# SiLU as one ScalarE function, a compact attention state, and later fills of the buckets, in a one-core attention and expert kernel

## The chip, the core and the metric

The kernel runs on one core of one Trainium2 chip. Its engines are TensorE (PE, with weight loads shown as PEld), VectorE (DVE), ScalarE (ACT), GpSimd (POOL) and SyncE (SP), which issues most transfers. The metric is the time of one execution on the device in microseconds; lower is better. A time of the kernel is a median of several runs; the profile shows one more execution by itself, whose time is given beside its span.

## The reference

Three stages follow each other. The state of the first is 48 x 48 for each of 4 x 8 heads; x then has 3072 rows (tokens) of 384.

```python
# 1: attention with a decayed state; q, k, v, alpha: (4, 8, 768, 48)
for t in range(768):
    state = alpha[:, :, t, :, None] * state + k[:, :, t] (x) v[:, :, t]
    y[:, :, t] = q[:, :, t] @ state
# 2: x: (3072, 384); w_gate, w_val: (384, 1536); w_out: (1536, 384)
xn = x / sqrt(mean(x * x) + 1e-6) * rms_g
g = xn @ w_gate
x = (g / (1 + exp(-g)) * (xn @ w_val)) @ w_out
# 3: one of 8 experts for each row; w1: (8, 384, 1024); w2: (8, 1024, 384)
logits = x @ r_gate
e = argmax(logits);  p = exp(logits - max);  p = p / (sum(p) + 1e-9)
out[row] = p[e] / (1 + exp(-(x @ r_ogate)[e])) * (relu(x @ w1[e]) @ w2[e])
```

The weights of stage 2 arrive as 64-bit floats.

## The kernel before

**Tiles.** The 768 steps of a batch are cut into six chunks of 128, so that there are 24 tiles of 128 rows. Three tiles make a group of 384 rows, and there are eight groups. A tile of attention has five stages: `score` (products `ps_s` of keys and queries, 16 matmuls, masked by DVE into `P0` and `P1`), `ktr` (keys turned on PE, copied by ACT to `kn`), `outp` (`ps_y`: queries times the old state plus the masked scores times `v`, then the RMS norm), `state` (`ps_st`: keys times values, added to the state) and `xtr` (the normed rows turned, and split by ACT and DVE into a high part `xh` and a rest `xl`, which PE multiplies separately). Ahead of `score` stands the preparation of a tile: loads `blk_a`, `blk_q`, `blk_k`, a turn of `alpha` on DVE (`aT`, L340), a running product, and scaled `qT`, `kT` and `en`, the decay over the whole chunk.

**The state.** Each tile of the state is [128, 4, 96]: four pairs of heads, of which the first head of a pair has partitions 0 to 47 and columns 0 to 47, the second partitions 64 to 111 and columns 48 to 95; the remainder is zero, so that one matmul serves a pair. POOL fills three such tiles with zeros at the start (L188). In `score`, DVE multiplies the state by `en`, one instruction for each of the two blocks (L393). In `state`, DVE adds `ps_st` block by block (L454), or, for the first chunk of a batch, DVE or ACT copies it (L450, L452).

**Stage 2** works on blocks of 128 of the 1536 inner columns, 12 for each group, so 96 in all. `m_gate` makes `ps_g` with nine matmuls (L571); ACT writes tanh(g/2) to `tt` (L562), and DVE makes (tt + 1) g of it (L563). `m_val` makes `ps_v`; DVE multiplies tt by half of it (L582) and ACT copies the result to its high part `hh` (L585). `m_low` takes the rest `hl` on DVE (L591). `m_out` multiplies both by the block of `w_out`, nine matmuls of 400 columns (L605), in which the last three read `hl`; it adds up in three banks `ps_o`.

**Weights of stage 2.** They are loaded as pairs of 32-bit words (`stg`, L485), converted by DVE in three operations (the first of them L490) into a buffer `F` or `Fo` (three of them, under the tag `cF`), and split by ACT and DVE. This is finished some 170 us into the run. For that reason the first two groups are interleaved: runs s = 0 to 3 are group 0 blocks 0 to 5, group 1 blocks 0 to 5, group 0 blocks 6 to 11, group 1 blocks 6 to 11. From then on a group is one run.

**Routing.** `route_a` of a group takes the maximum and the exponentials of 8 logits per row, and the output gate as exp(-o), in short operations on DVE and ACT; `route_b` counts rows on PE, makes the rows' places `pos`, and POOL scatters the rows into `bucket` in DRAM (eight regions, one for each expert). `init_bucket` fills a region beforehand with empty rows by one transfer on SP (L689) from `zrow`. Group 0 is routed in run 3, each later group in the run behind its own, and the last one behind everything. Then stage 3 loads rows of an expert (`er`, L956), turns them on PE and multiplies (`ps_h` L571, `ps_b` L1007).

**What sets the order.** The program is written in loops that interleave stages by due times; the first tiles follow a list in `CFG['START']`. A scheduler then places the instructions of each engine by simulated times, except for some that are pinned to the written order. Fills are pinned, at these lines of the loop over run s and step n, one for every second step of run 2:

```python
if s == 2 and (n - CFG['IB']) % 2 == 0 and 0 <= (n - CFG['IB']) // 2 < E:
    init_bucket((n - CFG['IB']) // 2)
```

Of the kernel before, what the change touches and what calls it, by code (L numbers as in the profile page):

```python
# [8 lines left out]
F32 = mybir.dt.float32  # L9
# [3 lines left out]
AF = mybir.ActivationFunctionType  # L13
# [38 lines left out]
def gla_glu_moe_kernel(  # L52
# [16 lines left out]
    nc = tc.nc  # L69
# [114 lines left out]
    place_of = [(t % BS, t // BS) if t < BS * NCH else (BS, t - BS * NCH) for t in range(NTILE)]  # L184
    state_of = []
    for i in range(BS):
        t_ = att.tile([P, NP, 2 * D], F32, name=f"state{i}")
        nc.gpsimd.memset(t_, 0.0)  # L188
        state_of.append(t_)

    vt = {}
    pre = {}
# [59 lines left out]
    def seat_of(t, nm, shape, bufs=1):  # L252
        if (t, nm) in SIDE:
            tag, i = SIDE[t, nm]
            if tag not in side:
                side[tag] = wpool.tile([P, 3, NP * P], F32, tag=tag, name="side")
            flat = side[tag][:, i, 0:shape[1] * (shape[2] if len(shape) > 2 else 1)]
            return flat.rearrange("p (a b) -> p a b", a=shape[1]) if len(shape) > 2 else flat
        return att.tile(shape, F32, tag=nm, name=nm, bufs=bufs)
# [113 lines left out]
    def stages(t):  # L373
        b, c = place_of[t]
        first, final = c == 0, c == NCH - 1
        en, qT, kT = pre[t]
        S_ = state_of[b % BS]
        rs = [slice(64 * hh, 64 * hh + D) for hh in range(2)]
        ds_ = [S_[rs[hh], :, hh * D:hh * D + D] for hh in range(2)]
        g, ti = divmod(t, GT)  # L380
        Pt = {}

        def score():
            ps = [bank([P, NP, P], "ps_s") for _ in range(2)]
            for p in range(NP):
                for hh in range(2):
                    r = slice(64 * hh, 64 * hh + D)
                    nc.tensor.matmul(ps[hh][:, p, :], lhsT=kT[r, p, :], rhs=qT[r, p, :], start=True, stop=True)  # L388

            def post():  # L390
                if not first:
                    for hh in range(2):
                        nc.vector.tensor_tensor(out=ds_[hh], in0=ds_[hh], in1=en[rs[hh]].to_broadcast([D, NP, D]),  # L393
                                                op=ALU.mult)
                mb = mask.to_broadcast([P, NP, P])
                for hh in range(2):
                    Ph = seat_of(t, f"P{hh}", [P, NP, P])
                    pace(f'Ph{t}', nc.vector.tensor_tensor(out=Ph, in0=ps[hh], in1=mb, op=ALU.mult))
                    Pt[hh] = Ph
            return post  # L400
        yield score

        def ktr():
            if final:
                return None
            ps = bank([P, NP, P], "ps_k")
            for p in range(NP):
                nc.tensor.transpose(ps[:, p, :], kT[:, p, :], ident)  # L408
            kn = seat_of(t, "kn", [P, H, D])
            nc.scalar.activation(kn, ps.rearrange("p a (h d) -> p (a h) d", h=2)[:, :, 0:D], AF.Copy)  # L410
            Pt["kn"] = kn
            return None
        yield ktr
# [23 lines left out]
        def state():  # L437
            if final:
                return None
            kn = Pt["kn"]  # L440
            ps = bank([P, NP, D], "ps_st")
            for p in range(NP):
                for hh in range(2):
                    nc.tensor.matmul(ps[64 * hh:64 * hh + D, p, :], lhsT=kn[:, 2 * p + hh, :],  # L444
                                     rhs=vt[t][:, 2 * p + hh, :], start=True, stop=True)

            def post():
                for hh in range(2):
                    if first and b < BS and SM[b] == "a":
                        nc.scalar.activation(ds_[hh], ps[rs[hh]], AF.Copy)  # L450
                    elif first:
                        nc.vector.tensor_copy(ds_[hh], ps[rs[hh]])  # L452
                    else:
                        nc.vector.tensor_tensor(out=ds_[hh], in0=ps[rs[hh]], in1=ds_[hh], op=ALU.add)  # L454
            return post
        yield state

# [97 lines left out]
    def m_gate(g, j):  # L555
        xh, xl = xT[g]
        ps = psM.tile([P, G], F32, tag="g", name="ps_g")
        mm3(ps, weight("wgh", j), weight("wgl", j), xh, xl)

        def post():  # L560
            tt = act.tile([P, G], F32, tag="t", name="tt")
            nc.scalar.activation(tt, ps, AF.Tanh, scale=0.5)  # L562
            nc.vector.scalar_tensor_tensor(out=tt, in0=tt, scalar=1.0, in1=ps, op0=ALU.add, op1=ALU.mult)  # L563
            hbuf[g, j] = tt
        return post

# [8 lines left out]
    def m_val(g, j):  # L575
        xh, xl = xT[g]
        ps = psM.tile([P, G], F32, tag="v", name="ps_v")
        mm3(ps, weight("wvh", j), weight("wvl", j), xh, xl)

        def post():  # L580
            tt = hbuf[g, j]
            nc.vector.scalar_tensor_tensor(out=tt, in0=tt, scalar=0.5, in1=ps, op0=ALU.mult, op1=ALU.mult)  # L582
            hh = act.tile([P, G], F32R, tag="hh", name="hh")
            hl = act.tile([P, G], F32R, tag="hl", name="hl")
            nc.scalar.activation(hh, tt, AF.Copy)  # L585
            hbuf[g, j] = (hh, hl, tt)
        return post
# [42 lines left out]
    def route_a(g):  # L630
# [6 lines left out]
        nc.vector.tensor_tensor(out=ex, in0=L, in1=mx.to_broadcast(bc), op=ALU.subtract)  # L637
        oh = small("oh", bc)
        nc.vector.tensor_scalar(out=oh, in0=ex, scalar1=0.0, scalar2=None, op0=ALU.is_ge)
        nc.scalar.activation(ex, ex, AF.Exp)  # L640
        nc.vector.tensor_tensor(out=oh, in0=oh, in1=rev8.to_broadcast(bc), op=ALU.mult)
        m8 = small("m8", [P, GT, 1])
        nc.vector.tensor_reduce(out=m8, in_=oh, op=ALU.max, axis=AX.X)
# [8 lines left out]
        nc.vector.tensor_tensor(out=sg, in0=oh, in1=O, op=ALU.mult)  # L652
        og = small("og", [P, GT, 1])
        nc.vector.tensor_reduce(out=og, in_=sg, op=ALU.add, axis=AX.X)
        nc.scalar.activation(og, og, AF.Exp, scale=-1.0)
        se = small("se", [P, GT, 1])
        nc.vector.tensor_reduce(out=se, in_=ex, op=ALU.add, axis=AX.X)
        rt[g] = (oh, ohb, ohc, m8, og, se)
# [1 line left out]
    def route_b(g):  # L660
# [6 lines left out]
            nc.tensor.matmul(ps[:, i, :], lhsT=ones_b, rhs=ohc[:, i - 1, :], start=False, stop=True)  # L667
        nc.tensor.matmul(ps[:, GT, :], lhsT=ones_b, rhs=ohc[:, GT - 1, :], start=True, stop=True)
        bc = [P, GT, E]
        nc.vector.tensor_scalar(out=se, in0=se, scalar1=1e-9, scalar2=None, op0=ALU.add)  # L670
        nc.vector.scalar_tensor_tensor(out=se, in0=og, scalar=1.0, in1=se, op0=ALU.add, op1=ALU.mult)
        nc.vector.reciprocal(out=R[:, :, DM:DM + 1], in_=se)
        nc.vector.tensor_copy(R[:, :, DM + 1:DM + 2], tokid[:, g * GT:g * GT + GT, :])
        rk = small("rk", bc)
        nc.vector.tensor_tensor(out=rk, in0=ps[:, 0:GT, :], in1=cnt.to_broadcast(bc), op=ALU.add)
# [11 lines left out]
    def init_bucket(e):  # L687
        tc.keep_in_program_order(
            nc.sync.dma_start(bucket[e * REG:e * REG + CMAX, :].rearrange("(p b) w -> p b w", p=P),  # L689
                              zrow.to_broadcast([P, CMAX // P, RW])))  # L690


    chunks = weight_chunks()
# [40 lines left out]
    def prep_step():  # L734
        if prep:
            prep.pop(0)()
# [91 lines left out]
    for s in range(4):  # L828
        N = 3 * (runs[s][2] - runs[s][1])
        paced[0] = CFG['K2'] if s else CFG['K1']  # L830
        for n in range(N):
# [22 lines left out]
            if s == 0 and done % NST == 0:  # L854
                while prep:
                    prep_step()
            if s == 2 and (n - CFG['IB']) % 2 == 0 and 0 <= (n - CFG['IB']) // 2 < E:
                init_bucket((n - CFG['IB']) // 2)
            if s == 3 and n == CFG['RA0']:
                route_a(0)  # L860
            if s == 3 and n == CFG['RB0']:
                route_b(0)


    BIG = float(1 << 20)
# [161 lines left out]
    for g in range(2, NG):  # L1027
# [14 lines left out]
        for n in range(3 * KF):  # L1042
# [3 lines left out]
            if done < (NTILE - GT) * NST and ((g - 1) * 3 * KF + n + 1 + CFG['LEADG']) * GT >= (done + 1 - GT * NST) * 3 * KF / NST:  # L1046
                post = stage()
                if post:
                    post()
            prep_step()  # L1050
            if n == CFG['RA']:
                route_a(g - 1)
            if n == CFG['RB']:
# [261 lines left out]
```

## Time and profile before

| | |
|---|---|
| three timed runs | 896.6, 899.89, 901.41 us (median 899.89) |
| the profiled execution | 895.87 us, of it 894.2 us span |
| busy in it: PE, DVE, ACT, POOL | 864.0, 559.9, 310.8, 141.9 us |
| mean granted clock of PE | 0.977 of full speed |

The span is the time from the first to the last instruction in the trace. Busy time is the sum over an engine's instructions; PE and PEld run beside each other. In a wait, the arrow names what ended it: `<-DVE hl L591` is a wait that ended with that write. In the windows and on the page, the granted clock is 1.00 at 2.4 GHz and 0.50 at 1.2 GHz, the two levels that occur.

### The profile page before, as it was taken

To read this page: it belongs to the slowest core of one execution; us is meant where nothing else is said; L and a number is where in the kernel's file an instruction comes from. 1 tells how busy PE (TensorE), PEld (TensorE's weight loads), DVE (VectorE), ACT (ScalarE), POOL (GpSimd) and SP (SyncE) were. 2 spreads that over 40 slices of the span, in tenths; PEclk is the share of its full clock that TensorE was granted. 3 is DMA by queue.
4 is the path that set the end of the run, shared out by engine and by line. 5 is a ranking of instruction groups with operands and counts; after the bars stand their busy time and mean duration, and the time that the engine had idled before them with its cause. 6 is when DMAs were issued, how large, how long until landed. Compare 5 with 4: busy or idle time off the path is not lost.

```text
span 894.2 us, 15813 instructions
## 1 busy us (share of the span) xinstructions
PE 864.0 (97%) x6048; PEld 821.6 (92%) x6048; DVE 559.9 (63%) x1295; ACT 310.8 (35%) x670; POOL 141.9 (16%) x177
## 2 busy tenths in 40 slices
PE   7989989999999999999999999999999999999994
PEld 6787889999999999999999999999998999999994
DVE  8689869977886776776677774354444433443330
ACT  1534534322323323332322332324224443444431
POOL 2100000001010010010010001012124343343341
PEclk8699999999999999999999999999999999999997
DMA  9826893312331231232222100005044363266510
GB/s 196 208 77 175 253 274 122 74 43 64 80 101 47 54 85 50 67 84 55 53 68 57 45 10 27 1 18 169 0 169 151 110 207 110 88 195 195 170 43 26
DMA packets 117485, 89.95 MB, mean 101 GB/s; under 512 B 49435, under 2 KB 112540, under 8 KB 117408
## 3 DMA queue, kind: packets, MB, share of 16 engines
q1 hardware_dynamic: 112944, 79.44, 32.8%
q0 software_dynamic: 4464, 9.48, 3.0%
q8 instruction: 48, 0.79, 0.4%
q14 instruction: 29, 0.24, 0.1%
HBM read 73.09 MB, written 16.07 MB: 100 GB/s over the span
## 4 chain that ended last, share of the span: by engine, by line
PE 70%; issue 4%; DMA 3%; DVE 2%; SPq 2%; POOL 1%; ACT 0%; POOLq 0%; DVEq 0%; ACTq 0%
PE ps_o L605 15%; PE ps_g L571 14%; PE ps_v L571 14%; PE ps_b L1007 10%; PE ps_h L571 9%; DMA st<-in_moe_w_dram 2%; PE ps_y L423 2%; PE ps_s L388 2%; PE ps_y L419 2%; SPq L875 1%; PE ps_st L444 1%; POOL out_dram L1023 1%; PE ps_t L971 1%; PE ps_k L408 1%; PE ps_x L468 1%
## 5 line engine op out<-in xcount | busy, mean ns | idle before, releaser
L585 ACT ACTIVATE hh<-tt 128x384 fp32r<-128x384 f32 x96 | 50.2, 523 | 167.6 <-DVE tt L582 166.4
L563 DVE SCALAR_TENSOR_TENSOR tt<-tt,ps_g 128x384 f32<-128x384 f32 x96 | 52.8, 550 | 72.0 <-ACT tt L562 71.5
L562 ACT ACTIVATE tt<-ps_g 128x384 f32<-128x384 f32 x96 | 47.1, 491 | 143.1 <-PE ps_g L571 140.3
L992 DVE SCALAR_TENSOR_TENSOR h<-ps_h,h 128x256 fp32r<-128x256 f32 (+6 forms) x72 | 37.9, 530 | 53.3 <-ACT h L991 53.2
L571 PE MATMUL ps_g<-xh,wgh 128*128 128x384 f32 x192 | 68.8, 359 | 1.4 <-ACT xh L475 0.7
L1007 PE MATMUL ps_b<-w2a,h 128*128 128x384 f32 (+2 forms) x336 | 67.5, 339 | 2.1 <-ACT h L991 2.1
L571 PE MATMUL ps_v<-xh,wvh 128*128 128x384 f32 x192 | 66.6, 347 | 0.8 <-ACT wvh L515 0.8
L605 PE MATMUL ps_o<-woh,hh 128*128 128x400 f32 x192 | 66.3, 354 | 0.0
L605 PE MATMUL ps_o<-wol,hh 128*128 128x400 f32 x192 | 66.3, 346 | 0.0
L571 PE MATMUL ps_g<-xl,wgh 128*128 128x384 f32 x192 | 65.7, 342 | 0.4 <-DVE xl L476 0.4
L605 PE MATMUL ps_o<-woh,hl 128*128 128x400 f32 x192 | 63.3, 347 | 2.8 <-DVE hl L591 2.8
L571 PE MATMUL ps_g<-xh,wgl 128*128 128x384 f32 x192 | 65.8, 343 | 0.0
L1007 PE MATMUL ps_b<-w2b,h 128*114 128x384 f32 (+3 forms) x336 | 65.0, 338 | 0.2 <-ACT h L991 0.2
L582 DVE SCALAR_TENSOR_TENSOR tt<-tt,ps_v 128x384 f32<-128x384 f32 x96 | 52.8, 550 | 19.8 <-PE ps_v L571 18.4
L571 PE MATMUL ps_v<-xh,wvl 128*128 128x384 f32 x192 | 65.0, 338 | 0.0
L591 DVE TENSOR_TENSOR hl<-tt,hh 128x384 fp32r<-128x384 f32 x96 | 53.3, 556 | 18.2 <-ACT hh L585 18.1
L571 PE MATMUL ps_v<-xl,wvh 128*128 128x384 f32 x192 | 64.5, 336 | 0.0
L430 POOL TENSOR_SCALAR ss<-ss 128x1 f32<-128x1 f32 x24 | 5.9, 245 | 365.5 <-ACT xn L429 358.1
L1007 PEld LDWEIGHTS ps_b<-w2a,h 128*128 128x128 f32 (+2 forms) x336 | 57.7, 181 | 3.4 <-ACT h L991 2.8
L1007 PEld LDWEIGHTS ps_b<-w2b,h 128*114 128x114 f32 (+3 forms) x336 | 57.6, 175 | 2.0 <-ACT h L991 0.6
L571 PE MATMUL ps_h<-x,w1b 128*128 128x456 f32 (+3 forms) x288 | 58.7, 344 | 0.0
L991 ACT ACTIVATE h<-ps_h 128x256 fp32r<-128x256 f32 (+6 forms) x72 | 33.4, 468 | 63.3 <-PE ps_h L571 63.1
(254 smaller groups left out, 2065.8 us busy)
## 6 DMA issues: line engine op xcount, KB each, us to landing
st<-in_moe_w_dram SPq DMA_DIRECT2D x64, 384.0 KB, 4.7
bucket<-zrow SPq DMA_DIRECT2D x8, 772.0 KB, 8.7
stg<-in_moe_w_gate_dram SPq DMA_DIRECT2D x12, 384.0 KB, 3.9
stg<-in_moe_w_val_dram SPq DMA_DIRECT2D x12, 384.0 KB, 4.5
stg<-in_moe_w_out_dram SPq DMA_DIRECT2D x12, 384.0 KB, 4.4
v<-in_v_dram SPq DMA_DIRECT2D x23, 192.0 KB, 3.1
blk_a<-in_alpha_dram SPq DMA_DIRECT2D x38, 96.0 KB, 2.2
blk_q<-in_q_dram SPq DMA_DIRECT2D x38, 96.0 KB, 2.2
```

The source lines that it names most:

```text
L388: nc.tensor.matmul(ps[hh][:, p, :], lhsT=kT[r, p, :], rhs=qT[r, p, :], start=True, stop=True)
L419: nc.tensor.matmul(ps[:, p * 2 * D:p * 2 * D + 2 * D], lhsT=qT[:, p, :], rhs=S_[:, p, :], start=(p == 0), stop=False, skip_group_check=True)
L562: nc.scalar.activation(tt, ps, AF.Tanh, scale=0.5)
L563: nc.vector.scalar_tensor_tensor(out=tt, in0=tt, scalar=1.0, in1=ps, op0=ALU.add, op1=ALU.mult)
L571: nc.tensor.matmul(ps, lhsT=a_[:, kc, :], rhs=b_[:, kc, :], start=(n == 0), stop=(n == 3 * KD - 1))
L582: nc.vector.scalar_tensor_tensor(out=tt, in0=tt, scalar=0.5, in1=ps, op0=ALU.mult, op1=ALU.mult)
L585: nc.scalar.activation(hh, tt, AF.Copy)
L591: nc.vector.tensor_tensor(out=hl, in0=tt, in1=f(hh), op=ALU.subtract)
L605: nc.tensor.matmul(obank[s][i], lhsT=a_[:, sl], rhs=weight(b_, j), start=(j == j0 and n == 0), stop=(j == j1 - 1 and n == 2))
L991: nc.scalar.activation(hh[:, 0, :], ps, AF.Relu)
L992: nc.vector.scalar_tensor_tensor(out=hh[:, 1, :], in0=ps, scalar=0.0, in1=f(hh[:, 0, :]), op0=ALU.max, op1=ALU.subtract)
L1007: ins = nc.tensor.matmul(ob2[u][i][0:r], lhsT=hh[:, a_, sl], rhs=we[p][b_][:, j, :], start=(j == 0 and m == 0), stop=(j == KF2 - 1 and m = ...
```

## The change

It has three parts, the first with a piece in the router.

- **SiLU.** ACT's function is now Silu itself, and L563 goes away; the multiplication by `ps_v` becomes a plain product. In the router the exponential of x is written as (1 + tanh(x/2)) / (1 - tanh(x/2)), three more DVE operations per group, and the output gate as half of 1 + tanh(o/2).
- **State.** It is kept compact, [128, 4, 48]: DVE multiplies and adds in one operation each where there were two, and ACT copies it for a batch's first chunk. A single tile `wide` in the old form, filled with zeros once, is written by two ACT copies ahead of `outp`. So that `ps_st` has all 128 partitions, `kn` keeps 64 columns per head instead of 48.
- **Fills.** The source is a copy `zero` in a `cF` buffer, made in run 3, and the eight fills are issued in run 3. The scheduler puts them behind the last conversion that used this buffer. Routing of group 0 goes from run 3 to group 2.

```diff
     for i in range(BS):
-        t_ = att.tile([P, NP, 2 * D], F32, name=f"state{i}")
+        state_of.append(att.tile([P, NP, D], F32, name=f"state{i}"))
+    wide = []
+    for i in range(1):
+        t_ = att.tile([P, NP, 2 * D], F32, name=f"wide{i}")
         nc.gpsimd.memset(t_, 0.0)
-        state_of.append(t_)
+        wide.append(t_)
...
-        S_ = state_of[b % BS]
+        Sc = state_of[b % BS]
+        S_ = wide[0]
...
                 if not first:
+                    nc.vector.tensor_tensor(out=Sc, in0=Sc, in1=en.to_broadcast([P, NP, D]), op=ALU.mult)
                     for hh in range(2):
-                        nc.vector.tensor_tensor(out=ds_[hh], in0=ds_[hh], in1=en[rs[hh]].to_broadcast([D, NP, D]),
-                                                op=ALU.mult)
+                        nc.scalar.activation(S_[rs[hh], :, hh * D:hh * D + D], Sc[rs[hh]], AF.Copy)
...
-            kn = seat_of(t, "kn", [P, H, D])
-            nc.scalar.activation(kn, ps.rearrange("p a (h d) -> p (a h) d", h=2)[:, :, 0:D], AF.Copy)
+            kn = seat_of(t, "kn", [P, H, 64])
+            nc.scalar.activation(kn, ps.rearrange("p a (h d) -> p (a h) d", h=2), AF.Copy)
...
-                    nc.tensor.matmul(ps[64 * hh:64 * hh + D, p, :], lhsT=kn[:, 2 * p + hh, :],
+                    nc.tensor.matmul(ps[64 * hh:64 * hh + 64, p, :], lhsT=kn[:, 2 * p + hh, :],
...
-                for hh in range(2):
-                    if first and b < BS and SM[b] == "a":
-                        nc.scalar.activation(ds_[hh], ps[rs[hh]], AF.Copy)
-                    elif first:
-                        nc.vector.tensor_copy(ds_[hh], ps[rs[hh]])
-                    else:
-                        nc.vector.tensor_tensor(out=ds_[hh], in0=ps[rs[hh]], in1=ds_[hh], op=ALU.add)
+                if first:
+                    nc.scalar.activation(Sc, ps, AF.Copy)
+                else:
+                    nc.vector.tensor_tensor(out=Sc, in0=ps, in1=Sc, op=ALU.add)
...
-            nc.scalar.activation(tt, ps, AF.Tanh, scale=0.5)
-            nc.vector.scalar_tensor_tensor(out=tt, in0=tt, scalar=1.0, in1=ps, op0=ALU.add, op1=ALU.mult)
+            nc.scalar.activation(tt, ps, AF.Silu)
...
-            nc.vector.scalar_tensor_tensor(out=tt, in0=tt, scalar=0.5, in1=ps, op0=ALU.mult, op1=ALU.mult)
+            nc.vector.tensor_tensor(out=tt, in0=tt, in1=ps, op=ALU.mult)
...
-        nc.scalar.activation(ex, ex, AF.Exp)
+        nc.scalar.activation(ex, ex, AF.Tanh, scale=0.5)
+        er_ = small("er_", bc)
+        nc.vector.tensor_scalar(out=er_, in0=ex, scalar1=-1.0, scalar2=1.0, op0=ALU.mult, op1=ALU.add)
+        nc.vector.reciprocal(out=er_, in_=er_)
+        nc.vector.scalar_tensor_tensor(out=ex, in0=ex, scalar=1.0, in1=er_, op0=ALU.add, op1=ALU.mult)
...
-        nc.scalar.activation(og, og, AF.Exp, scale=-1.0)
+        nc.scalar.activation(og, og, AF.Tanh, scale=0.5)
...
-                              zrow.to_broadcast([P, CMAX // P, RW])))
+                              zero.to_broadcast([P, CMAX // P, RW])))
...
-            if s == 2 and (n - CFG['IB']) % 2 == 0 and 0 <= (n - CFG['IB']) // 2 < E:
-                init_bucket((n - CFG['IB']) // 2)
-            if s == 3 and n == CFG['RA0']:
-                route_a(0)
-            if s == 3 and n == CFG['RB0']:
-                route_b(0)
+            if s == 3 and n == 0:
+                zero = act.tile([P, 1, RW], F32, tag="cF", name="zero", bufs=3)
+                nc.scalar.activation(zero, zrow, AF.Copy)
+            if s == 3 and n < 2 * E and n % 2 == 0:
+                init_bucket(n // 2)
...
+            if g == 2 and n in (1, 3):
+                (route_a, route_b)[n // 2](0)
```

On SP before, five fills of `bucket` stand between a load of `w_val` and the loads of the next tile and of `w_out`; a row is the line, the transfer, its destination and source, and its shape.

```order
L485 DMA stg<-in_moe_w_val_dram 128x3x256
L689 DMA bucket<-zrow 512x1x386 x5
L225 DMA blk_q<-in_q_dram 32x4x192
L485 DMA stg<-in_moe_w_out_dram 128x768
L325 DMA v<-in_v_dram 128x8x48
L485 DMA stg<-in_moe_w_gate_dram 128x3x256
```

In the changed kernel the last five fills stand behind a load of `v` and ahead of the `blk_a` of a later tile, with the loads of weights all issued.

```order
L229 DMA blk_q<-in_q_dram 32x4x160
L695 DMA bucket<-zero 512x1x386 x2
L329 DMA v<-in_v_dram 128x8x48
L695 DMA bucket<-zero 512x1x386 x3
L229 DMA blk_a<-in_alpha_dram 32x4x192
L229 DMA blk_a<-in_alpha_dram 32x4x160
```

The fills have moved past every `stg` load, to the loads for attention tiles of later groups.

On ACT before, ahead of the first gate, `xn` of the first tiles is scaled, a first state is copied in two parts, and `xh` stands ahead of two weight parts.

```order
L474 ACTIVATE xn<-ps_x,gT 128x128 x3
L450 ACTIVATE state_133<-ps_st 48x4x48 x2
L475 ACTIVATE xh<-xn 128x3x128
L515 ACTIVATE wgh<-F 128x3x128
L515 ACTIVATE wvh<-F 128x3x128
L562 ACTIVATE tt<-ps_g 128x384
```

In the changed kernel the same place reads:

```order
L475 ACTIVATE xn<-ps_x,gT 128x128 x3
L453 ACTIVATE state_132<-ps_st 128x192
L398 ACTIVATE wide_134<-state_131 48x4x48 x2
L516 ACTIVATE wgh<-F 128x3x128
L476 ACTIVATE xh<-xn 128x3x128
L516 ACTIVATE wvh<-F 128x3x128
L563 ACT_TABLE_LOAD
L563 ACTIVATE tt<-ps_g 128x384
```

The two copies into `wide` and one weight part have come ahead of `xh`, and a table load ahead of the first gate.

On DVE before, in the routing of the last group, the steps to the rows' places `pos` follow one `h` of stage 3 in a row.

```order
L992 SCALAR_TENSOR_TENSOR h_7300<-ps_h,h_7300 128x256
L675 TENSOR_TENSOR rk<-ps_r,cnt 128x24
L676 TENSOR_TENSOR rk<-rk,oh 128x24
L682 TENSOR_TENSOR cnt<-cnt,ps_r 128x8
L678 TENSOR_REDUCE pf<-rk 128x3
L879 SCALAR_TENSOR_TENSOR key_7234<-cnt,rev_75 128x8
L681 TENSOR_TENSOR pos<-pf,m_7182 128x3
```

In the changed kernel:

```order
L997 SCALAR_TENSOR_TENSOR h_7237<-ps_h,h_7237 128x256
L681 TENSOR_TENSOR rk<-ps_r,cnt 128x24
L682 TENSOR_TENSOR rk<-rk,oh 128x24
L688 TENSOR_TENSOR cnt<-cnt,ps_r 128x8
L684 TENSOR_REDUCE pf<-rk 128x3
L884 SCALAR_TENSOR_TENSOR key_7171<-cnt,rev_75 128x8
L997 SCALAR_TENSOR_TENSOR h_7258<-ps_h,h_7258 128x256
L687 TENSOR_TENSOR pos<-pf,m_7119 128x3
```

One more `h` stands between the count and `pos`.

## Rows read from the trace of the kernel before

**Rows 1.** Page, part 1: busy us, share of the span, instructions by engine

```profile
PE 864.0 (97%) x6048; PEld 821.6 (92%) x6048; DVE 559.9 (63%) x1295; ACT 310.8 (35%) x670; POOL 141.9 (16%) x177
```

**Rows 2.** Windows: start:end, us, busy PE, PEld, DVE, ACT, POOL, PEclk, DMA, GB/s

```profile
20.00:30.00 10.00, 10.00 (x77) 8.29 (x78) 8.22 (x18) 4.00 (x11) 1.59 (x3) 0.50 0.98 178
...
120.00:140.00 20.00, 17.06 (x90) 16.24 (x90) 14.48 (x33) 6.10 (x14) 0.00 (x0) 0.91 0.82 238
...
400.00:500.00 100.00, 100.00 (x753) 95.32 (x752) 68.08 (x157) 30.06 (x71) 6.86 (x13) 1.00 0.24 61
```

**Rows 3.** Waits of PE: us in all, how often, the longest

```profile
PE ps_o L605 <- DVE hl L591: 2.8, 1, 2.8
...
PE ps_v L571 <- ACT wvh L515: 0.8, 1, 0.8
...
PE ps_v L571 <- DVE tt L582: 0.4, 1, 0.4
```

**Rows 4.** Timeline of PE: start, us, instruction, [wait before it and its releaser]

```profile
125.13 0.82 PE L605 MATMUL ps_o<-woh,hl 128*128 128x400 f32 x3 [2.83 <-DVE hl L591]
...
127.28 0.52 PE L571 MATMUL ps_g<-xl,wgh 128*128 128x384 f32 x1
```

**Rows 5.** Timeline of DVE, ahead of that wait's end

```profile
124.25 0.36 DVE L490 TENSOR_SCALAR Fo<-stg 128x384 int32<-128x384 int32 x1 [5.62 <-DMA stg<-in_moe_w_out_dram]
```

**Rows 6.** Timeline of SP, 104 to 114 us

```profile
104.50 6.09 SPq L689 DMA_DIRECT2D bucket<-zrow  x5
...
112.16 1.21 SPq L485 DMA_DIRECT2D stg<-in_moe_w_out_dram  x1
```

**Rows 7.** Page, part 6: DMA issues, KB each, median us from issue to landing

```profile
bucket<-zrow SPq DMA_DIRECT2D x8, 772.0 KB, 8.7
```

**Rows 8.** Timeline of SP and DVE, 208 to 225 us

```profile
208.13 1.74 SPq L225 DMA_DIRECT2D blk_a<-in_alpha_dram  x4
...
223.60 1.10 DVE L340 STREAM_TRANSPOSE aT<-blk_a 128x512 f32<-128x512 f32 x1
```

**Rows 9.** Groups by line and form: count, busy us, mean ns, idle before and releaser

```profile
L563 DVE SCALAR_TENSOR_TENSOR tt<-tt,ps_g 128x384 f32<-128x384 f32 x96 | 52.8, 550 | 72.0 <-ACT tt L562 71.5
...
L450 ACT ACTIVATE state<-ps_st 48x192 f32<-48x192 f32 x2 | 0.6, 321 | 0.0
...
L142 ACT ACT_TABLE_LOAD x1 | 1.3, 1283 | 0.8 <-PEq L1299 0.8
```

**Rows 10.** Timeline of ACT, its first `tt`

```profile
52.00 0.50 ACT L562 ACTIVATE tt<-ps_g 128x384 f32<-128x384 f32 x1 [2.45 <-PE ps_g L571]
```

**Rows 11.** Timeline of POOL, DVE and PE at the start, to 50 us

```profile
3.02 1.13 POOL L188 MEMSET state<- 128x384 f32 x3
...
38.82 1.47 DVE L452 COPY state<-ps_st 48x192 f32<-48x192 f32 x4
...
47.25 1.57 PE L388 MATMUL ps_s<-qT,kT 48*128 48x128 f32 x16 [2.47 <-DVE qT L313]
```

**Rows 12.** Critical chain, 170 to 211 us: start, us, what

```profile
171.48 1.07 PE ps_y L423 x32
...
198.26 0.49 PE ps_st L444 x16
198.75 1.83 PE ps_o L605 x9
...
208.81 1.64 PE ps_o L605 x9
```

**Rows 13.** Timeline of DVE behind the last routing

```profile
652.83 0.43 DVE L992 SCALAR_TENSOR_TENSOR h<-ps_h,h 128x256 fp32r<-128x256 f32 x1
...
662.07 0.17 DVE L964 CAST ix<-er 128x2 int32<-128x2 f32 x1 [2.41 <-DMA er<-bucket]
```

**Rows 14.** Timeline of DVE and PE, 632 to 637 us

```profile
632.59 0.56 DVE L591 TENSOR_TENSOR hl<-tt,hh 128x384 fp32r<-128x384 f32 x1 [0.59 <-ACT hh L585]
...
636.00 0.35 PE L605 MATMUL ps_o<-wohe,hh 128*128 128x400 f32 x1
```

More of the change, by code (lines that the diff above doesn't have):

```diff
@@ L376, in stages @@
         en, qT, kT = pre[t]
-        S_ = state_of[b % BS]
+        Sc = state_of[b % BS]
+        S_ = wide[0]
         rs = [slice(64 * hh, 64 * hh + D) for hh in range(2)]
-        ds_ = [S_[rs[hh], :, hh * D:hh * D + D] for hh in range(2)]
         g, ti = divmod(t, GT)
@@ L669, in route_b @@
         bc = [P, GT, E]
-        nc.vector.tensor_scalar(out=se, in0=se, scalar1=1e-9, scalar2=None, op0=ALU.add)
-        nc.vector.scalar_tensor_tensor(out=se, in0=og, scalar=1.0, in1=se, op0=ALU.add, op1=ALU.mult)
-        nc.vector.reciprocal(out=R[:, :, DM:DM + 1], in_=se)
+        nc.vector.tensor_scalar(out=se, in0=se, scalar1=1e-9, scalar2=2.0, op0=ALU.add, op1=ALU.mult)
+        nc.vector.reciprocal(out=se, in_=se)
+        nc.vector.scalar_tensor_tensor(out=R[:, :, DM:DM + 1], in0=og, scalar=1.0, in1=se, op0=ALU.add, op1=ALU.mult)
         nc.vector.tensor_copy(R[:, :, DM + 1:DM + 2], tokid[:, g * GT:g * GT + GT, :])
```

## The prediction

> **What bounds the kernel now.** I read the page first, then the windows, then the waits of TensorE (PE), then the timelines around the longest of them. On the page the reader is to see that PE is busy for 864.0 of 894.2 us and VectorE (DVE) for 559.9 [rows 1]. So the change, which takes work from DVE, can only pay where PE stands still, or runs at a low clock, because of DVE. The windows say where that is: from 400 to 500 us PE is busy for all of 100 us at clock 1.00 [rows 2], and nothing DVE saves there moves the end. From 120 to 140 us it is busy for 17.06 us only, at a mean granted clock of 0.91 [rows 2]. Between 20 and 30 us it is busy throughout, but at 0.50, which is 1.2 of 2.4 GHz [rows 2].
>
> The list of PE's waits shows how little there is to win. One wait of 2.8 us stands out, of the out projection for `hl` from DVE; behind it come six short ones between 0.8 and 0.4 us [rows 3] (0.8, 0.7, 0.6, 0.5, 0.4, 0.4, together 3.4 us). The rest lies in the first 48 us and in the last 24.
>
> The cause of the long wait can be followed. PE resumes at 125.13 us after 2.83 us [rows 4]. `hl` is the instruction behind `Fo<-stg` on DVE, and that one stood 5.62 us until 124.25 us for a weight transfer from `w_out` [rows 5]. SyncE (SP) had issued that transfer at 112.16 us, right after five fills of buckets that held its queue for 6.09 us from 104.50 us on [rows 6]; each fill moves 772 KB and lands after 8.7 us in the median [rows 7]. A fill is early work for a late stage, and here it pushed a transfer that was due. Afterwards PE's matmuls ran at half clock for a while [rows 4]: a mean of 0.91 over 20 us is 20 x 0.09 = 1.8 us of lost full-clock time, that is 3.6 us at half clock.
>
> **The change part by part.**
>
> *Fills.* In the new order no fill stands ahead of a weight transfer any more. Two go behind the `blk_k` loads of a later tile, one behind a `v`, five ahead of a `blk_a`. That takes away the 2.8 us, and of the 1.8 us of clock I take 1.5 (bounds 0 and 1.8). What is late next there? DVE loses a 5.6 us hole, and PE's next wait in the list is 0.8 us. The cost at the new place: five fills go out ahead of a `blk_a` load. In the trace of before that load is issued at 208.13 us and its transpose is at 223.60 us [rows 8], 15.5 us later, and five fills took 6.09 us of queue; their bytes have to fit into the rest. I put this at 0, and its failure is a rival below.
>
> *SiLU.* It takes 96 DVE operations of 550 ns, 52.8 us of DVE [rows 9], and puts none in their place: the ScalarE (ACT) operation before becomes another function on the same tile. From 160 us on, PE hides all of it. Earlier it shortens the queue that the short waits stand in. Six waits of 3.4 us in all: four of the six are for DVE, one of them is for exactly the removed operation, two for ACT behind DVE. I take 1.9 of the 3.4 (bounds 0 and 3.4), a little over half, since the scheduler refills DVE with conversions at once.
>
> *The table load.* ACT's new order has one more table load, ahead of the first SiLU; its one load of before took 1283 ns [rows 9]. Before its first `tt`, ACT stood 2.45 us for PE [rows 10], so the load fits: 0. By the Trainium skill ("ScalarE: Activation LUTs", What ACT_TABLE_LOAD costs) a switch is about 2.66 us with its drain; no run here shows the drain, and by that figure the sum would be 0.2 us worse, as an estimate.
>
> *Compact state.* In the start phase DVE loses four copies of the first states (1.47 us) [rows 11] and one of two multiplications; ACT takes three copies and then, per tile, two spreads. PE stood 2.47 us at 47.25 us for `qT` from DVE [rows 11], so up to 1.8 us of this could come forward. But ACT now has the spread and a weight conversion ahead of `xh`, on which the first gate waits; two of its copies of the nearest shape cost 2 x 321 ns [rows 9], and they wait for DVE's scan. POOL's first matter is smaller: three state fills of 1.13 us become one of about 0.38 [rows 11], in front of the tiles for which PE waits first; between 0 and 0.75 us of that counts. For the start together I take 1.0 us of gain (bounds 2.2 gain, 0.5 loss), and 0.4 (0 to 0.8) for the clock after a shorter gap. Behind the start, 20 tiles with two spreads are 20 x 2 x 0.321 = 13 us more of ACT, beside 583 us in which it is idle (894.2 less its 310.8 [rows 1]): 0. The wider `kn` has 64 weight columns where 48 stood. The nearest rows are `ps_y` with 64 columns, 1.07 us for 32 matmuls, 33.4 ns each, and `ps_st` with 48, 0.49 for 16, 30.6 ns [rows 12]: 2.8 ns x 16 x 20 = 0.9 us at most, 0 at least; I take 0.5.
>
> *The order.* All instructions are placed anew. A run of nine out-projection matmuls takes 1.83 us behind a group of the other kind and 1.64 behind its own [rows 12], so each return costs 0.19 us. I counted the returns in both orders: 161 before, 168 after. 7 x 0.19 = 1.3 us loss (bounds 0 and 1.3).
>
> *Router.* Three small DVE operations more per group, hidden by PE in seven of eight. In the last one the position `pos` starts the scatter, the load of rows and PE's transposes. At 662.07 us DVE had waited 2.41 us for those rows [rows 13], and PE starts on them at once. Ahead of `pos` now stand three operations of at most 0.17 us and one `h` of 0.43 [rows 13]: between 0 and 0.9, I take 0.6 us loss. Routing group 0 later costs nothing: its scatter still has 400 us.
>
> **Sum.** -2.8 - 1.5 - 1.9 - 1.0 - 0.4 + 0.5 + 1.3 + 0.6 = -5.2 us. Against the profiled execution (895.87 us; span 894.2 and 1.7 around it) that is 890.7. That execution was faster than all three timed ones (median 899.89); the mean of the four is 898.4, and 898.4 - 5.2 gives **893.2 us**, which I forecast. All bounds at their best give -11.2, at their worst +0.8 with the fills still gone and the table load as the row has it.
>
> **The rivals.**
>
> *A, the clock of the start.* PE runs at half clock for all of the window from 20 to 30 us [rows 2]. If the shifted start gets the full clock some microseconds earlier, each microsecond at half clock that was busy gives back 0.5. Ten of them are 5 us, so about 888; together with the good ends of the other terms about 885. For it: PE is busy there, and DVE is ahead of it. Against: the same PE order stands there as before.
>
> *B, the fills bite again.* If five fills land later than 15.5 us after they are issued, the transposes of `blk_a` hold DVE as `Fo` did, and the 2.8 and 1.5 us come back: 897.5. For it: the fills are moved, not removed, and in before the transfer behind five of them took from 112.16 to 124.25 us. Against: there the loads were competing with weights on the way, here they are not.
>
> *C, slower: ACT's queue.* ACT works in order. If each spread waits for DVE's multiplication, or for the reads of the one shared `wide` tile, SiLU and `hh` wait behind it. The slack can be read: `hl` ends at 632.59 + 0.56 = 633.15 us and the matmuls that read it follow those that start at 636.00 us [rows 14], 2.85 us later. The pair itself is 0.64 us, so it decides only from a wait of 2.2 us on; then PE would lose up to the pair's 0.64 us in each of 20 tiles, 12.8 us: 906. Against: the multiplication stands two stages ahead of the use.
>
> *D, nothing.* The hole closes, and the new order opens holes of the same size elsewhere in the first 160 us, where DVE is nearly full: 898 to 900.
>
> **How the numbers follow.** Forecast 0.60, A 0.13, B 0.12, C 0.08, D 0.07. Half a per cent of the median is 4.5 us, about what a measurement of this kernel can tell from no change: faster means under 895.4, slower over 904.4. Of the forecast's 0.60, 0.44 lie under 895.4, since 5.2 is close to the border; with A that is 0.57. The rest of the forecast, B and D, with a little for C at half its price, is 0.34; slower 0.09. The range takes in the forecast's own ends (888 to 898), B, and half of A: 885.5 to 899.5. It leaves out C, the far end of A and part of D.
>
> **What would show it.** Right: no wait of PE over 1 us between 50 and 600 us, a clock of 1.00 from 120 to 140 us, DVE's wait for a `w_out` transfer gone, DVE lower by the 53 us of SiLU and somewhat more by the state's operations (about 500 us), and ACT higher by the spreads and copies (about 325). B shows as a DVE wait for `blk_a` or `blk_q` between 170 and 230 us, C as waits of PE for `hl` spread over 20 tiles with ACT waiting for `wide`. The tail term shows as a wait of PE for `er` just after the last scatter. I am wrong in substance if the hole at 122 us is gone and the time is not: then the path through it was DVE's and not the transfer's.

## The result and the profile after

The changed kernel took 889.79 us (median of four; 888.62 to 891.49) against 899.41 us before (median of four; 896.6 to 901.41). The ratio is 0.9897, with an interval of 0.9864 to 0.993: 9.3 us faster, between 6 and 12. Forecast were 893.2 us in a range of 885.5 to 899.5, and that the kernel gets faster. The time lies in the range, but 5.2 us of gain were worked out and more than 9 came.

The profiled execution of the changed kernel took 891.49 us, 889.8 of it span. It was the slowest of its four, while the one of before, 895.87 us, was faster than every timed one. The two profiles differ by 4.4 us, less than half of what the medians differ by. That gap is the main question of what follows.

The page after, busy us, share and instructions by engine (answers to [rows 1]):

```profile
PE 866.0 (97%) x6048; PEld 826.0 (93%) x6048; DVE 502.3 (56%) x1181; ACT 329.0 (37%) x714; POOL 139.9 (16%) x175
```

DVE fell by 57.6 us and ACT rose by 18.2. PE's busy time rose by 2 us; what fell is its idle time, from 30.2 (894.2 less 864.0) to 23.8 us.

Windows of the changed kernel, in the columns of [rows 2]:

```profile
20.00:30.00 10.00, 10.00 (x78) 8.29 (x77) 9.38 (x21) 4.53 (x12) 0.82 (x3) 0.50 1.10 178
60.00:80.00 20.00, 19.64 (x145) 17.23 (x142) 18.15 (x42) 8.28 (x21) 0.75 (x2) 0.91 0.52 136
120.00:140.00 20.00, 20.00 (x124) 19.88 (x123) 18.70 (x43) 9.30 (x22) 0.00 (x0) 1.00 0.49 154
```

From 120 to 140 us PE now works throughout at full clock. But a mean of 0.91, the same loss of 1.8 us, stands from 60 to 80 us instead, where before had 1.00, and the window from 20 to 30 us is at 0.50 as before.

All waits of PE between 50 and 600 us in the changed kernel (answers to [rows 3]):

```profile
PE ps_v L571 <- ACT wvh L516: 0.2, 1, 0.2
PE ps_s L392 <- ACT xn L475: 0.2, 1, 0.2
```

The wait for `hl` is gone, and so are the short ones; DVE has no wait for a transfer in that stretch either. By stretches, PE's idle time in us, from the windows of each trace (the two columns in the middle are experiments below):

| us | before | before, second profile | fills alone | after |
|---|---|---|---|---|
| 0 to 60 | 9.4 | 11.2 | 9.8 | 8.8 |
| 60 to 100 | 2.1 | 2.1 | 2.1 | 0.4 |
| 100 to 140 | 3.1 | 6.5 | 0.1 | 0.0 |
| 140 to 600 | 0.8 | 0.8 | 0.4 | 0.0 |
| 600 to 870 | 2.9 | 3.8 | 3.8 | 2.6 |
| from 870 | 12.0 | 12.0 | 12.4 | 12.0 |
| all | 30.2 | 36.4 | 28.7 | 23.8 |

### The profile page after: what moved, and what is told of

Read it like the earlier page. It is cut to its first block, busy times and chain, and to the rows that moved or that the text cites. A ratio compares the mean times of both kernels' runs of the same rounds, so it can differ in the third digit from the quotient of the medians.

```text
span 889.8 us, 15748 instructions
## 1 busy us (share of the span) xinstructions
PE 866.0 (97%) x6048; PEld 826.0 (93%) x6048; DVE 502.3 (56%) x1181; ACT 329.0 (37%) x714; POOL 139.9 (16%) x175
## 3 DMA queue, kind: packets, MB, share of 16 engines
q1 hardware_dynamic: 112944, 79.44, 33.5%
## 4 chain that ended last, share of the span: by engine, by line
PE 86%; issue 4%; DMA 3%; DVE 2%; POOL 1%; ACT 1%; SPq 1%; POOLq 0%; ACTq 0%; DVEq 0%
PE ps_o L605 18%; PE ps_g L571 18%; PE ps_v L571 17%; PE ps_b L1012 8%; PE ps_h L571 7%; PE ps_s L392 4%; PE ps_y L427 3%; DMA st<-in_moe_w_dram 3%; PE ps_y L423 2%; PE ps_st L448 1%; PE ps_k L412 1%; PE ps_l L503 1%; PE ps_x L469 1%; SPq L880 1%; PE ps_n L248 1%
## 5 line engine op out<-in xcount | busy, mean ns | idle before, releaser
L582 DVE TENSOR_TENSOR tt<-tt,ps_v 128x384 f32<-128x384 f32 x96 | 52.8, 550 | 129.5 <-PE ps_v L571 122.6
L563 ACT ACTIVATE tt<-ps_g 128x384 f32<-128x384 f32 x96 | 47.2, 492 | 127.5 <-PE ps_g L571 119.6
L996 ACT ACTIVATE h<-ps_h 128x256 fp32r<-128x256 f32 (+6 forms) x72 | 33.4, 468 | 63.5 <-PE ps_h L571 57.5
L571 PE MATMUL ps_h<-x,w1a 128*128 128x256 f32 (+3 forms) x288 | 53.4, 327 | 0.0
```

The lines of the kernel that those rows point to most:

```text
L563: nc.scalar.activation(tt, ps, AF.Silu)
L571: nc.tensor.matmul(ps, lhsT=a_[:, kc, :], rhs=b_[:, kc, :], start=(n == 0), stop=(n == 3 * KD - 1))
L582: nc.vector.tensor_tensor(out=tt, in0=tt, in1=ps, op=ALU.mult)
L996: nc.scalar.activation(hh[:, 0, :], ps, AF.Relu)
```

## The experiments

**The parts by themselves.** Theory T was mine: the transfer of `w_out`, queued behind five fills, makes the stall. Rival L: DVE is too full, and the fills only show it. Four kernels tell them apart, on one chip with the kernel before; of each edit the main lines are shown, and `...` marks what is left out. First, the fills and the routing of group 0 alone:

```diff
+            if s == 3 and n == 0:
+                zero = act.tile([P, 1, RW], F32, tag="cF", name="zero", bufs=3)
+                nc.scalar.activation(zero, zrow, AF.Copy)
+            if s == 3 and n < 2 * E and n % 2 == 0:
+                init_bucket(n // 2)
...
```

> The kernel before with the fills and the routing of group 0 moved as in the change, SiLU and state as before. Theory T (the transfer of w_out behind five fills makes the stall): PE's wait of 2.8 us for hl and the half clock at 126 us go, 2.8 + 1.5 = 4.3 us less than before, ratio 0.995; the short waits for DVE, 3.4 us, stay. Rival L (DVE was too full, and the fills only showed it): under 1 us less, and another wait of 2 to 3 us between 60 and 140 us.

Measured: 892.98 us against 901.64, ratio 0.9899 (0.9876 to 0.9922). As a ratio to the kernel before, the fills by themselves give as much as the whole change. No wait of PE over 0.8 us is left between 60 and 240 us, and from 120 to 140 us PE works throughout at full clock:

```profile
120.00:140.00 20.00, 20.00 (x122) 19.92 (x121) 19.23 (x45) 9.28 (x21) 0.00 (x0) 1.00 0.45 144
```

T holds in kind, but its gain of 4.3 us was too small: the medians differ by 8.7.

Second, SiLU and the router's tanh alone:

```diff
-            nc.scalar.activation(tt, ps, AF.Tanh, scale=0.5)
-            nc.vector.scalar_tensor_tensor(out=tt, in0=tt, scalar=1.0, in1=ps, op0=ALU.add, op1=ALU.mult)
+            nc.scalar.activation(tt, ps, AF.Silu)
...
```

> The kernel before with SiLU as one ScalarE function and the router's tanh, fills and state as before. T: a wait of PE of 2 to 3 us for hl stays, since four or five fills still stand ahead of a w_out load; 1.9 us less by the short waits, with 0.6 back at the last routing, ratio 0.9985. L: the stall goes with DVE's load, 4 us or more less, ratio 0.9955 or lower.

Measured: 902.96 us, ratio 1.0013 (0.9999 to 1.0027). DVE loses 40 us of work, and the time does not move. The stall is there, at another instruction and longer than in the first profile of before; the longest wait of PE in this kernel:

```profile
PE pt L527 <- DVE Fo L496: 4.9, 1, 4.9
```

L falls with this: an emptier DVE waits for the same transfer, and what it saves ahead of the transfer it spends in waiting for it.

Third, the compact state alone:

```diff
+                    nc.vector.tensor_tensor(out=Sc, in0=Sc, in1=en.to_broadcast([P, NP, D]), op=ALU.mult)
                     for hh in range(2):
-                        nc.vector.tensor_tensor(out=ds_[hh], in0=ds_[hh], in1=en[rs[hh]].to_broadcast([D, NP, D]),
-                                                op=ALU.mult)
+                        nc.scalar.activation(S_[rs[hh], :, hh * D:hh * D + D], Sc[rs[hh]], AF.Copy)
...
```

> The kernel before with the compact state alone. T: 1.0 us less at the start and 0.4 of clock, 0.5 back for the wider kn, so 0.9 us less, ratio 0.999; the stall of 2.8 us stays. Rival C (ACT's queue): slower by 3 us or more, with PE waits behind ACT.

Measured: 897.62 us, ratio 0.9953 (0.9938 to 0.9969), more than the 0.9 us expected. In its profile PE waits hardly at all from 60 to 100 us, and then longer for `hl`:

```profile
PE ps_o L606 <- DVE hl L592: 5.1, 1, 5.1
```

The two cancel there: idle from 60 to 140 us is 5.3 us, and 5.2 in the first profile of before. So the profile does not show where its 4 us in the median come from; that stays open.

Fourth, the changed kernel with the old fills:

```diff
-            if s == 3 and n < 2 * E and n % 2 == 0:
-                init_bucket(n // 2)
+            if s == 2 and (n - CFG['IB']) % 2 == 0 and 0 <= (n - CFG['IB']) // 2 < E:
+                init_bucket((n - CFG['IB']) // 2)
...
```

> The changed kernel with fills and the routing of group 0 back at their places of before. T: the stall comes back, so it is 4.3 us slower than the changed kernel, some 5 us faster than before, ratio 0.994. L: as fast as the changed kernel, ratio 0.990, with no wait of PE over 1 us from 60 to 140 us.

Measured: 899.48 us, ratio 0.9981 (0.9964 to 0.9997), and the stall is back:

```profile
PE pt L528 <- DVE Fo L497: 6.2, 1, 6.2
```

Without the moved fills the change is worth 1.7 us, less than the state alone: the parts do not add up. T holds, but its price of 4.3 us is half of the 8.7 that the moved fills gave.

**What SiLU and the state add behind the moved fills.** Three kernels in another session, again beside the kernel before (898.91 us there): the changed kernel, fills with SiLU, fills with the state. Their edits are the hunks above, put together.

> The changed kernel once more, beside the next ones on the same chip. If the fills carry all (theory F, from the run with the fills alone, ratio 0.990), it lies within 1.5 us of it: ratio 0.989 to 0.991. If SiLU and state pay on top of the fills, as my sum has it (1.9 + 1.0 + 0.4 less 0.5, 1.3 and 0.6, so 0.9 us), 0.989.

> The kernel before with fills and SiLU changed, state as before. PE's order has 173 returns to large matmuls, where before has 161 and the changed kernel 168. Theory R (each return costs 0.19 us): 5 x 0.19 = 1 us slower than the changed kernel, and about 1 us more for the start's state copies on DVE; ratio 0.992. Rival: SiLU's relief of DVE decides, ratio as the changed kernel or lower, 0.989.

> The kernel before with fills and state changed, SiLU as before. 161 returns. R: 7 x 0.19 = 1.3 us faster than the changed kernel, less what DVE's short waits cost (up to 1.9): ratio 0.988 to 0.991. Rival (DVE's load still matters behind the fills): slower than the changed kernel by 2 us or more, 0.992 or higher.

Measured: 891.34 us (ratio 0.992, 0.9899 to 0.994) for the changed kernel, 894.09 (0.9943, 0.9923 to 0.9963) with SiLU, 892.78 (0.993, 0.9909 to 0.995) with the state. Beside each other, all but one of the six executions of the changed kernel lie under all six of fills with SiLU; those of fills with the state overlap with it. So behind the moved fills and SiLU the state is worth some 2.8 us, and what SiLU is worth behind the other two (1.4 us in the medians) is not clear of the noise. What both are worth over the fills alone is not settled, since no session has the two kernels beside each other: the medians say 1.6 to 3.2 us (891.34 and 889.79 against 892.98), the ratios to the kernel before nothing (0.992 and 0.9897 against 0.9899). The profiles show what stands against what: the changed kernel has 4.9 us less idle time of PE than the fills alone (5.7 in its second profile) and 3.3 us more busy time (2.9).

The order of the three does not follow the returns to large matmuls (168, 173, 161): fills with the state, with the fewest, was forecast 1.3 us faster than the changed kernel and measured 1.4 us slower. Theory R alone does not explain them.

**Queue or bytes.** Five fills hold SP's queue for 6.09 us [rows 6], and they also put 3.9 MB into the transfer engines. A first kernel issued them from ACT:

```diff
-            nc.sync.dma_start(bucket[e * REG:e * REG + CMAX, :].rearrange("(p b) w -> p b w", p=P),
+            nc.scalar.dma_start(bucket[e * REG:e * REG + CMAX, :].rearrange("(p b) w -> p b w", p=P),
```

> The kernel before, with its fills at the same steps but issued by ScalarE instead of SyncE. Theory Q (the stall is SyncE's queue, held for 6 us by five fills, so that the w_out load is issued late): the stall goes, ratio 0.990 to 0.993. Theory D (the stall is the fills' 6 MB in the transfer engines, which all loads share): the stall of PE stays at 3 us or more, ratio 0.998 or higher, and the w_out load takes longer from issue to landing.

Measured: 892.87 us, ratio 0.9935 (0.9911 to 0.9958), without the stall. Between queue and bytes it decides nothing, since in ACT's order the fills came late, so that they were moved in time as well:

```profile
L689 ACTq DMA_DIRECT2D bucket<-zrow x8: 541/551/650, 148.9 to 177.4; - x8
```

But it answers another question, which the kernel with the fills alone leaves open: here the routing of group 0 stayed in run 3, and the stall is gone all the same. The two that follow keep early transfers near the loads of weights. For the second, SP is held without bytes, with the real fills late:

```diff
+            if s == 2 and n % 2 == 0 and n < 2 * E:
+                for _ in range(8):
+                    tc.keep_in_program_order(nc.sync.dma_start(scrap[next(nscrap)], zrow[:, 0, 0:8]))
```

> The kernel with the fills alone moved, and in place of the eight early fills 64 transfers of 4 KB on SyncE, in bunches of 3 to 12 ahead of the loads of weights: SyncE's queue is held for some 64 x 0.4 = 25 us in all, with 0.26 MB. Q (the queue holds back the w_out load): waits of DVE for stg of 3 us or more, ratio 0.995 or higher. D (the bytes in the transfer engines do): as with the fills alone moved, ratio 0.989 to 0.993, no wait of PE over 1.2 us from 60 to 140 us.

Measured: 896.17 us against 901.94, ratio 0.9938 (0.9915 to 0.996), between the two theories; the interval overlaps with that of the fills alone, so that the time by itself does not show what the queue costs. A bunch of six held SP for 2.86 us ahead of a load of `w_val`, and DVE then waited 3.4 us for that load; rows of the timelines of SP and DVE:

```profile
119.83 2.86 SPq L861 DMA_DIRECT2D scrap<-zrow  x6
122.78 1.45 SPq L487 DMA_DIRECT2D stg<-in_moe_w_val_dram  x1
```

```profile
127.45 0.36 DVE L492 TENSOR_SCALAR F<-stg 128x384 int32<-128x384 int32 x1 [3.37 <-DMA stg<-in_moe_w_val_dram]
```

The load itself landed within 4.7 us of its issue; it had only been issued late. PE then waited 1.1 us for `hl`. For the third, the bytes stay and SP is left free:

```diff
-            nc.sync.dma_start(bucket[e * REG:e * REG + CMAX, :].rearrange("(p b) w -> p b w", p=P),
+            nc.gpsimd.dma_start(bucket[e * REG:e * REG + CMAX, :].rearrange("(p b) w -> p b w", p=P),
```

> The kernel before, with its fills issued by GpSimd. In the new order the first four stand behind the norm of the tile that was at 107 us in the kernel before, the other four behind 173 us. D: four fills, 3 MB, still stand in the transfer engines beside the loads due at 112 to 125 us, though SyncE is free: a wait of PE for DVE or Fo of 2 us or more near 120 us, ratio 0.995 or higher. Q: no such wait, ratio 0.989 to 0.993.

Measured: 900.93 us, ratio 1.0009 (0.9985 to 1.0033): as slow as before, with a wait of PE of 4.0 us behind DVE. POOL issued four fills at 108.61 us; from the timelines of POOL, SP and DVE, and from the view of the loads' line from 100 to 140 us:

```profile
108.61 3.22 POOL L689 DMA_DIRECT2D bucket<-zrow  x4
```

```profile
112.28 1.58 SPq L485 DMA_DIRECT2D stg<-in_moe_w_val_dram  x1
```

```profile
127.37 0.36 DVE L490 TENSOR_SCALAR F<-stg 128x384 int32<-128x384 int32 x1 [6.31 <-DMA stg<-in_moe_w_val_dram]
```

```profile
DMA to landing us min/median/max: 2.9/3.8/15.1
```

SP had issued the load of `w_val` at 112.28 us, with no fill ahead of it, and DVE had its data 15.1 us later, where the median load of that stretch took 3.8. So D holds: the bytes alone are enough for the stall. The queue alone gave a wait of 1.1 us, with SP held for some 31 us in all where the eight fills held it for 8. The Trainium skill bears on this ("DMA: Bandwidth & Descriptors", Issuing engines are not separate DMA queues): transfers of all issuing engines run on the same 16 transfer engines and interleave, and another issuer saves only the time to issue. This trace agrees, with 15.1 us for that load.

A rival would be the number of packets, not of bytes. Part 3 of the pages (queue, packets, MB, share) speaks against it; the small transfers on SP and the fills from POOL:

```profile
q1 hardware_dynamic: 122160, 79.71, 34.3%
q0 software_dynamic: 6000, 15.81, 5.5%
```

Before, these queues had 112944 packets and 4464. So the small transfers added 9216 packets with 0.27 MB and cost PE little, while the fills from POOL made 1536 packets with 6.3 MB and brought the stall.

**Where the missing 4 us were.** The first profile of before was too fast for its medians, and so the kernel was profiled once more.

> The kernel before once more, for a second profile. Theory V (the stall varies from execution to execution, and the first profile, faster than every timed run, showed a short one): with a time near 899, the stall at 120 us is 5 to 8 us instead of 2.8. Rival W (the missing 4 to 5 us lie elsewhere, in the clock or in the end): the stall is 2.8 us again, and the time lost stands in other windows.

This execution took 904.31 us, 902.6 of it span. It is the slowest of this kernel on record, as the first profile is the fastest, so the two show the ends and not the middle. Its longest wait of PE, its window, and the timelines of SP and DVE (answers to [rows 2 to 6]):

```profile
PE ps_o L605 <- DVE hl L591: 6.1, 1, 6.1
```

```profile
120.00:140.00 20.00, 13.93 (x68) 13.36 (x67) 9.48 (x21) 4.36 (x10) 0.00 (x0) 0.83 0.94 242
```

```profile
107.00 6.95 SPq L689 DMA_DIRECT2D bucket<-zrow  x5
116.95 0.95 SPq L485 DMA_DIRECT2D stg<-in_moe_w_out_dram  x1
...
119.00 6.46 SPq L485 DMA_DIRECT2D stg<-in_moe_w_gate_dram  x1
...
131.97 0.37 SPq L485 DMA_DIRECT2D stg<-in_moe_w_gate_dram  x1
```

```profile
129.71 0.36 DVE L490 TENSOR_SCALAR Fo<-stg 128x384 int32<-128x384 int32 x1 [8.87 <-DMA stg<-in_moe_w_out_dram]
```

The same chain as in the first profile, only longer: PE waits 6.1 us instead of 2.8, and the clock behind it is 0.83 instead of 0.91, a loss of 3.4 us instead of 1.8. These two make 3.3 + 1.6 = 4.9 of the 8.4 us between the two spans; 1.8 more is idle time of PE ahead of 60 us. V holds: the stall varies from one execution to the next, and the first profile had caught a short one. By the prediction's way of pricing, stall and clock cost 2.8 + 1.8 = 4.6 us in the first profile and 6.1 + 3.4 = 9.5 in this one; the 8.7 us of the fills alone lie between. The fills themselves were slower here, 12.8 us to landing in the median against 8.7 [rows 7]; the page's part 6:

```profile
bucket<-zrow SPq DMA_DIRECT2D x8, 772.0 KB, 12.8
```

A single load of `w_gate`, which takes SP 0.37 us elsewhere, took 6.46 us to issue here, and 4.71 in the first profile; with the fills on POOL no load of weights took SP more than 1.58. So the fills in SP's own queue seem to hold SP up longer than by their own issue; why, no run here shows. The spread says too that the stall varies. Beside each other, the kernel before took 897.72 to 904.1 us in 27 runs, the one with its fills late 891.68 to 893.58 in six.

**The width of kn.** PE's groups of 16 `ps_st` had grown, and so the changed kernel was run with 48 columns again where a state is only added to:

```diff
-            nc.scalar.activation(kn, ps.rearrange("p a (h d) -> p (a h) d", h=2), AF.Copy)
+            kw = 64 if first else D
+            nc.scalar.activation(kn[:, :, 0:kw], ps.rearrange("p a (h d) -> p (a h) d", h=2)[:, :, 0:kw], AF.Copy)
...
-                    nc.vector.tensor_tensor(out=Sc, in0=ps, in1=Sc, op=ALU.add)
+                    for r in rs:
+                        nc.vector.tensor_tensor(out=Sc[r], in0=ps[r], in1=Sc[r], op=ALU.add)
...
```

> The changed kernel with 48 columns of kn per head again wherever the state is added to (64 only for the first chunks, which fill the whole compact state), and DVE's addition in two halves: 16 tiles. Theory K (the wider kn costs PE 0.11 us per tile: a group of 16 ps_st takes 0.60 us in the changed kernel, 0.49 before): 16 x 0.11 = 1.8 us less than the changed kernel, groups of 0.49 us in the dense stretch, about 888.5 us or a ratio to before of 0.988. Rival (PE hides it, or DVE's 16 more operations of 0.35 us cost as much): as the changed kernel, 890 to 891 us, ratio 0.990 to 0.992.

One group in the chain of waits, of the changed kernel and then of this one:

```profile
194.44 0.60 PE ps_st L448 x16
```

```profile
192.88 0.49 PE ps_st L449 x16
```

The 0.11 us per tile are real, and PE's busy time fell from 865.6 (the changed kernel's second profile) to 863.9 us. The kernel's time does not clearly follow: 891.17 us (890.02 to 892.41), ratio to before 0.9876 (0.9855 to 0.9898). The ratio is the one that theory K forecast, the time is the rival's; both lie within the noise of the changed kernel's 0.9897 and 0.992, which were measured in other sessions. In its profile PE waited 1.2 us for the rows of an expert, and was idle for 3.4 us from 600 to 700 us; the changed kernel's second profile has 0.3 and 1.8. Whether it beats the changed kernel is not settled.

## Why the prediction was right, and where it was not

**The stall.** Right in mechanism, mis-sized by half. The place, the transfer, the fills ahead of it and the clock behind were as read, and moving the fills removes them. But -2.8 and -1.5 were taken from one execution, the fastest of all that were seen, although the prediction itself noted that it was faster than all three timed ones. It corrected the base for that (898.4 instead of 895.87) and kept the price of the stall. Against the one other execution that was profiled, the stall and its clock make up 4.9 of 8.4 us. The fills alone gave 8.7 us where 4.3 were forecast.

**The range.** That the time lay in it was in part luck. Stall and clock had at most 2.8 + 1.8 = 4.6 us in the prediction's bounds, and gave 8.7; the room for the rest was there because the range reached down for the good ends of the other terms and for half of rival A, and neither is what came. (The terms at their best make -11.0, and not -11.2.)

**The clock.** The half clock at 126 us went, as forecast, but in both profiles of the changed kernel one of the same cost came between 60 and 80 us; the second profile:

```profile
60.00:80.00 20.00, 19.62 (x116) 17.02 (x116) 19.44 (x46) 7.72 (x20) 0.74 (x2) 0.91 0.54 142
```

In this term nothing was won against the first profile of before. PE had stood still for only 0.4 us in the 4 us ahead of that half clock, and the fills with the state have 1.00 in the same window; why it comes, no run here shows.

**The rest of the sum.** Short waits, start, `kn`, order and tail were put at -1.9 - 1.0 - 0.4 + 0.5 + 1.3 + 0.6 = -0.9 us; between the fills alone and the whole the medians differ by 1.6 to 3.2, the ratios by nothing. From 60 to 100 us PE's idle time fell by 1.7 us, so the short waits were near their value. The start gave 0.6 us of idle time against the first profile of before; the 0.4 for its clock is not shown, since the mean clock of the first 60 us is 0.74 in one profile of the changed kernel and 0.77 in the other, and 0.77 before. There PE waits 0.5 us for `qT`, but 1.5 for `xh`, behind the two copies into `wide`, and 1.4 for `kn`:

```profile
PE ps_g L571 <- ACT xh L476: 1.5, 1, 1.5
PE ps_st L448 <- ACT kn L414: 1.4, 1, 1.4
```

**The order.** The 1.3 us for seven more returns are not shown: the three kernels with late fills did not follow that price.

**kn** was too cheap. The bound of 0.9 us came from `ps_y`, the same form at 33.4 ns each [rows 12]; a `ps_st` of 64 columns takes 0.60/16 = 37.5 ns, so that 20 tiles cost 20 x 0.11 = 2.2 us of PE, outside my bounds. How much of it the kernel's time pays is open.

**The table load** was free, as forecast; it ended 2.12 us before its function's data came:

```profile
48.64 1.28 ACT L563 ACT_TABLE_LOAD   x1
52.05 0.49 ACT L563 ACTIVATE tt<-ps_g 128x384 f32<-128x384 f32 x1 [2.12 <-PE ps_g L571]
```

**The tail.** PE waits 0.5 us for the rows of an expert behind the last routing (0.3 in the second profile), where 0.6 was forecast:

```profile
PE ps_t L976 <- DMA er<-bucket: 0.5, 1, 0.5
```

**Rival A** (an earlier full clock at the start gives 0.5 us for each busy microsecond) falls in this form. Executions of the kernel before whose mean clock was 0.989 to 0.992, some 12 us of clock above the usual 0.976, took 897.19 to 903.02 us; the usual ones took 896.8 to 904.1. These executions have no profile, so where the clock was higher is not seen; but the only stretch at half clock in any profile that is long enough to hold those 12 us is the one before 40 us. So there, it seems, PE's clock does not set the pace; this is argued, not shown.

**Rival B** (the fills bite at `blk_a`) did not happen. The last five hold SP for 1.22 and 5.68 us, a little longer than before, and the data still come in time; timelines of SP and DVE after (answers to [rows 8]):

```profile
197.31 5.68 SPq L695 DMA_DIRECT2D bucket<-zero  x3
204.52 2.54 SPq L229 DMA_DIRECT2D blk_a<-in_alpha_dram  x4
```

```profile
218.56 1.10 DVE L344 STREAM_TRANSPOSE aT<-blk_a 128x512 f32<-128x512 f32 x1
```

From issue to use are 14 us, and DVE did not wait.

**Rival C** (ACT's queue and the one `wide`) did not happen either: the spreads stood 13.7 us in all for PE's reads and 6.4 for DVE's product, and no wait of PE behind 50 us came of it.

```profile
L398 ACT ACTIVATE wide<-state 48x192 f32<-48x192 f32 x40 | 14.4, 361 | 20.4 <-PE ps_y L423 13.7 <-DVE state L396 6.4
```

**Rival D** (new holes of the same size) did not happen: PE's idle time fell. For SiLU alone, where the fills stay, the time did not move either, but there the hole is the old one, made by the same transfer.

## What to carry to other kernels

A bulk transfer that nobody waits for yet belongs behind the last small transfer that somebody waits for; moving it to another issuing engine at nearly the same time did not help here, since its bytes alone were enough to delay the load. SiLU's work, saved ahead of a late transfer, was lost in the wait for it, so take the transfer away first and measure the rest afterwards. Where one profile is faster than every timed run, the price of a stall that hangs on a transfer is probably too low: profile again before pricing it.

## What the hardware showed that was not expected

A single load that SP issues in 0.37 us took 6.46 us while fills were under way, and beside four fills from POOL a load that SP had issued took 15.1 us, where the median of its stretch was 3.8. The mean granted clock of an execution said little of its time: 0.99 and 0.976 went with the same times.
